# A soft-capped attention and spectral mixing kernel: weight splits and row sums of the first batch move between engines and steps, and the last batch's squares go out on two queues

## Chip, core and metric

The kernel runs on one core of a Trainium2 chip. The time is device microseconds of one execution. Five instruction streams matter: TensorE (PE, with its weight loads PEld), VectorE (DVE), ScalarE (ACT), GpSimd (POOL, nearly unused here) and SyncE (SP), which issues nearly all transfers. Each stream is executed in the order in which it is written; the streams wait for each other through semaphores.

## What is computed

```python
# q, k, v: (8 batches, 12 heads, 448 tokens, 64); x has 768 columns
scores = cap * tanh(q @ k^T / sqrt(64) / cap)
attn   = exp(scores - max) / (sum(exp(scores - max)) + 1e-9)
x      = heads side by side of (attn @ v)                   # (8, 448, 768)
theta  = x @ w_theta
zr, zi = x * cos(theta), x * sin(theta)
y      = w_tok_r @ zr + w_tok_i @ zi                         # over the tokens
u      = x + y
out    = u + max(u @ w_ch, 0)
```

## The kernel before

Attention is cut into 48 **units** of two heads, six units to a batch. A **step** s starts the scores of unit s and finishes unit s-1. Steps 0 to 7 do attention alone (table FRONT); from step 8 on, six steps do attention of one batch and, beside it, the mixing of an earlier one (PARTS, and OTHER for the first two steps and the last batch). Every step is a string of words, executed in order, and each word issues instructions on one engine or two. So the order on each engine is the order of the words. The words that matter here:

- `A`, `B`: scores of the unit's two halves on PE (lines "s", L216); both write the same PSUM tile, so `B` waits for the tanh of `A` (`tA`, L221) and the next `A` for `tB`. `eA`, `eB`: exponentials on ACT (L227). `V`: attn times v on PE (L259), with `cV` its copy on ACT (L265).
- `R`: row sums on PE by ones (L278), `I`: reciprocal on DVE (L301) and four transfers that spread it (bc, L305), `N` or `n`: the multiplications by it on DVE (L309). `aA`, `aB`: DVE adds the four 112x896 pieces of a unit's exponentials into `ps` (L249 once, L252 twice), after which `R` needs 2 matmuls for a unit instead of 8. Units under DIRECT have no such additions: units 0 to 5 are summed in pairs straight from the exponentials, units 6 up to DIRECT one at a time.
- `w0`, `w1`, `w2`: steps of the weights as listed in WEIGHTS: `>ch2` loads block 2 of w_ch, `*ch2` scales it on ACT (L110), `ch2` splits it on DVE into a high and a low part (L118 to L127; the rounding to the high part, L123, is on ACT for all blocks of w_ch).
- Mixing of column block j: `T` theta on PE (L328 to L330), `y` two copies on ACT (L350, L351), `d` three operations on DVE (L356 to L358), `sc` cosine and sine of two blocks on ACT (L363, L364; they need another function table than tanh and exp), `r` products with x on DVE (L368), `f` transposition inside 32x32 tiles on DVE (L372), `D` the **square** of two blocks: 16 transfers between partition groups inside `g_sb` (L381), `h`, `l` high and low parts of the transposed blocks on ACT and DVE (zh L386, zl L392; "a" the first four token chunks, "b" the other three), `M` the mixing matmuls (mx, 12 for "a", 9 for "b"), `m` their addition to x, `u` the split of u (us), `C` the channel matmuls (ch), `c` the last addition (L413) and the transfer of a block to the output (L414).

Square 0 goes from blocks 0 and 1 of `g_sb` to 6 and 7, square 1 from 2 and 3 to where square 0 came from, square 2 from 4 and 5 to 2 and 3. Transfers use eight landing semaphores in turn, in program order: one waits until the transfer eight before it has landed, and until what it overwrites was read.

Of the kernel before, what the change touches and what calls it, by code (L numbers as in the profile page):

```python
# [12 lines left out]
F32 = mybir.dt.float32  # L13
# [4 lines left out]
ALU = mybir.AluOpType  # L18

P = 128  # L20
# [5 lines left out]

FIRST = 8

DIRECT = 10

FILL = {"before the branch": 8, "first scores": 2, "half": 8, "slot": 10}

# [4 lines left out]
def softcap_attn_then_spectral_mix(ctx, tc, qk2, v, cap, w_theta, w_tok, w_ch, outT):  # L37
    nc = tc.nc
# [90 lines left out]
    def room_g(at):  # L129
# [3 lines left out]
            return raw, st[:, 2 * DM :].rearrange("p (j n) -> p j n", j=NJ)  # L133
        return room

    def room_t(i, name):
        def room():
            raw = g_sb[:, (12 + 2 * i) * S : (14 + 2 * i) * S]
            t = wk.tile([P, S], F32, tag="zl", name=f"{name}_t", bufs=2)
            return raw.rearrange("p (n two) -> p n two", two=2), t  # L140
        return room
# [3 lines left out]
    def weight_steps():  # L145
        for m in range(NJ):
            ms = slice(m * P, (m + 1) * P)
            steps["th", m] = Split(room_g((0, 6 * S)[m % 2]), w_theta[m], wth_h[:, :, ms], wth_l[:, :, ms])
            steps["ch", m] = Split(room_g((0, 6 * S, 8 * S, 0, 8 * S, 0)[m]), w_ch[m], wch_h[:, :, ms], wch_l[:, :, ms], True)
        for c in range(NC2):  # L150
            steps["tk", c] = Split(room_t(c % 2, f"swk{c}"), w_tok[c], wtk_h[:, c], wtk_l[:, c])

# [8 lines left out]
    }  # L161

    def weights(s, pos):
# [210 lines left out]
    def carry(b, i):  # L374

        at = 4 * S * i
        to = 4 * S * (i - 1) if i else 12 * S
        z, t = (g_sb[:, n : n + 4 * S].rearrange("p (c m d) -> p c m d", m=4, d=32) for n in (at, to))
        for m in range(4):
            for d in range(4):  # L380
                nc.sync.dma_start(t[32 * m : 32 * m + 32, :, d, :], z[32 * d : 32 * d + 32, :, m, :])  # L381

    def z_high(b, j, h):
        c0, c1 = ((0, 4), (4, NC2))[h]
# [25 lines left out]

    def chan_out(b, m):
        x = X.pop((b, m))
        nc.vector.scalar_tensor_tensor(x, acc_of.pop(("ch", b, m))[:, :S], 0.0, x, op0=ALU.max, op1=ALU.add)  # L413
        nc.sync.dma_start(outT[b, m * P : (m + 1) * P, :], x)  # L414

    FRONT = "A tA w0 eA V cV v R0 B tB R1 q w1 n I eB aA aB w2 x"
    PARTS = (
# [8 lines left out]
    )  # L426
    OTHER = {
        (0, 0): "A tA V cV w0 v R I B tB q P w1 eA T0 y0 d0 aA eB T1 y1 d1 sc0 T2 y2 r0 r1 f0 f1 d2 w2 D0",
        (0, 1): "A tA V cV N w0 v R I aB- B tB q P w1 T3 y3 d3 sc1 eA T4 r2 r3 f2 f3 D1 y4 d4 eB T5 aA aB y5 d5 w2",
        (B - 2, 4): "V cV u3 u4 u5 R I C0 c0 C1 X0 X1 c1 C2 X2 X3 c2",  # L430
        (B - 2, 5): "N X4 X5 T0+ y0+ d0+ T1+ y1+ d1+ sc0+ T2+ r0+ r1+ f0+ f1+ D0+ y2+ d2+ T3+ y3+ d3+ sc1+ T4+ r2+ r3+ f2+ f3+ D1+ y4+ d4+"
                    " T5+ y5+ d5+ sc2+ C3 c3 r4+ r5+ f4+ f5+ D2+ C4 c4 h0a+ l0a+ h0b+ l0b+ h1a+ C5 c5",
        (B - 1, 0): "M0a l1a h1b M0b l1b h2a m0 u0 M1a l2a h2b M1b l2b h3a m1 u1 M2a l3a h3b M2b l3b h4a m2 u2 M3a l4a h4b M3b l4b h5a"
                    " m3 u3 M4a l5a h5b M4b l5b m4 u4 M5a M5b m5 u5 C0 c0 C1 c1 C2 c2 C3 c3 C4 c4 C5 c5",
    }
# [1 line left out]
    def pipeline(general):  # L437
# [2 lines left out]
        load_qk(1)  # L440
        for step in (("tk", 0), ("tk", 1)):
            steps[step].load()

        def run(s, b, word):
            if word.endswith("+"):
# [23 lines left out]
            elif word == "cV":  # L469
                if done:  # L470
                    av_out(k)
            elif word == "v":
                if s + 1 < NS:
                    load_v(s + 1)
            elif name == "R":
                if done:
                    sums(k, (0, 1) if i is None else (i,))
            elif word == "I":
                if done:
                    invert(k)  # L480
            elif word == "q":
                if s + 2 <= WHOLE:
                    load_qk(s + 2)
            elif word == "P":
                if WHOLE <= s + 1 < NS:
                    prep(s + 1)
            elif name == "w":
                weights(s, "abc"[i])
            elif word == "N":
                norm(s - 3)  # L490
                norm(s - 2)
            elif word == "n":
                for n in {4: (0, 1), 5: (2, 3), 7: (4, 5)}.get(s, ()):
                    norm(n)
            elif word == "x":
                for j in {6: range(4), 7: range(4, NJ)}.get(s, ()):
                    split_x(0, j, "xs")
            elif name == "u":
                split_x(b, i, "us")
            elif name == "X":  # L500
                if b + 1 < B:
                    split_x(b + 1, i, "xs")
            elif name in ("h", "l", "M"):
                {"h": z_high, "l": z_low, "M": mix}[name](b, i, half)
            else:
                {"T": theta, "y": turns, "d": reduce, "sc": sincos, "r": rotate, "f": flip, "D": carry, "m": mix_out, "C": chan,
                 "c": chan_out}[name](b, i)
# [63 lines left out]
```

## Time and profile before

| | |
|---|---|
| three runs | 941.32, 944.65, 946.21 us (median 944.65) |
| the profiled execution | 941.22 us, its span 939.4 us, mean clock of PE 0.996 of full |
| busy share of the span | PE 98%, PEld 70%, DVE 73%, ACT 66%, POOL 0% |
| the chain that ended last | PE 73%, ACT 15%, DVE 6%, SP's queue 3%, DMA 1% |

The span is measured from the first to the last instruction; 1.8 us of the execution lie outside it. The share of the chain tells which engine the end waited for at each moment; a busy PE is nearly everywhere on it, so the places to look at are those where PE waits.

### The profile page before, as it was taken

What the parts mean: (1) busy time and instruction counts of PE and PEld (TensorE: products, weight loads), DVE (VectorE), ACT (ScalarE), POOL (GpSimd) and SP (SyncE); (2) the same over time, 40 slices, a digit from 0 to 9 for tenths busy, and PEclk for the clock granted to TensorE, in tenths of its full rate; (3) what the DMA queues carried; (4) which work ended last, traced back from release to release, by engine and by line L of the source; (5) the groups of instructions that cost most, each with busy time, mean ns of one, the idle gap of its engine ahead of it and who ended that gap; (6) DMA issues with size and microseconds to landing.
All of it is one profiled execution on the core that took longest, in us unless ns stands there. A gap on an engine that the chain in (4) does not pass through costs nothing.

```text
span 939.4 us, 12874 instructions
## 1 busy us (share of the span) xinstructions
PE 916.8 (98%) x4912; PEld 660.9 (70%) x4912; DVE 682.9 (73%) x914; ACT 617.6 (66%) x644; POOL 0.4 (0%) x6
## 2 busy tenths in 40 slices
PE   8999989999999999999999999999999999999997
PEld 4224657667776787777677776776877777789887
DVE  5898756997876679666887568775787568965741
ACT  7988696567954688656976479645895569753420
POOL 0000000000000000000000000000000000000000
PEclk9999999999999999999999999999999999999999
DMA  7664155422642235332452325422353333411521
GB/s 267 200 186 128 34 123 132 121 98 72 126 89 79 82 65 120 78 108 70 86 102 67 101 62 107 117 78 71 67 119 80 91 96 76 77 32 48 92 52 62
DMA packets 208774, 90.66 MB, mean 97 GB/s; under 512 B 182464, under 2 KB 194752, under 8 KB 208704
## 3 DMA queue, kind: packets, MB, share of 16 engines
q1 hardware_dynamic: 208704, 89.76, 38.3%
q8 instruction: 40, 0.66, 0.3%
q14 instruction: 30, 0.25, 0.1%
HBM read 45.68 MB, written 11.01 MB: 60 GB/s over the span
## 4 chain that ended last, share of the span: by engine, by line
PE 73%; ACT 15%; DVE 6%; SPq 3%; DMA 1%; issue 1%; DVEq 0%; ACTq 0%
PE a L259 10%; PE s L216 10%; PE mx L403 7%; PE mx L401 7%; PE mx L402 7%; PE ch L328 6%; PE ch L329 6%; PE ch L330 6%; ACT p L221 5%; PE th L328 4%; PE th L329 4%; PE th L330 4%; SPq L381 3%; ACT p L227 2%; PE r L278 2%; ACT L221 2%
## 5 line engine op out<-in xcount | busy, mean ns | idle before, releaser
L221 ACT ACTIVATE p<-s,qscale 112x1792 f32<-112x1792 f32 x96 | 168.5, 1755 | 124.2 <-PE s L216 122.6
L227 ACT ACTIVATE p<-p,cap_sb 112x1792 f32<-112x1792 f32 x96 | 170.2, 1785 | 0.4
L259 PE MATMUL a<-p,v 112*64 112x448 f32 x768 | 155.1, 546 | 3.7 <-ACT p L227 3.7
L259 PEld LDWEIGHTS a<-p,v 112*64 112x64 f32 x768 | 50.7, 136 | 91.0 <-issue 74.9
L328 PE MATMUL ch<-us,wch_h 128*128 128x448 f32 x288 | 107.1, 372 | 0.0
L328 PE MATMUL th<-xs,wth_h 128*128 128x448 f32 x288 | 107.0, 371 | 0.0
L329 PE MATMUL ch<-us,wch_h 128*128 128x448 f32 x288 | 105.5, 366 | 0.0
L329 PE MATMUL th<-xs,wth_h 128*128 128x448 f32 x288 | 105.5, 366 | 0.0
L330 PE MATMUL ch<-us,wch_l 128*128 128x448 f32 x288 | 105.4, 366 | 0.0
L330 PE MATMUL th<-xs,wth_l 128*128 128x448 f32 x288 | 105.3, 366 | 0.0
L252 DVE TENSOR_TENSOR ps<-ps,p 112x896 f32<-112x896 f32 x76 | 82.8, 1089 | 2.2
L301 DVE RECIPROCAL ri<-r 128x448 f32<-128x448 f32 x24 | 70.9, 2954 | 17.2 <-PE r L278 17.2
L403 PE MATMUL mx<-wtk_h,zl_False 128*128 128x448 f32 x192 | 71.4, 372 | 3.2 <-DVE zl_False L392 2.5
L401 PE MATMUL mx<-wtk_h,zh_False 128*128 128x448 f32 x192 | 72.0, 375 | 0.1
L402 PE MATMUL mx<-wtk_l,zh_False 128*128 128x448 f32 x192 | 70.2, 366 | 0.0
L368 DVE TENSOR_TENSOR g_sb<-g_sb,x 128x896 f32<-128x896 f32 x48 | 50.7, 1086 | 22.3 <-ACT g_sb L364 22.3
L413 DVE SCALAR_TENSOR_TENSOR x<-ch,x 128x448 f32<-128x448 f32 x48 | 29.8, 620 | 51.1 <-PE ch L330 51.1
L328 PEld LDWEIGHTS ch<-us,wch_h 128*128 128x128 f32 x288 | 54.2, 188 | 10.3 <-issue 5.3
L328 PEld LDWEIGHTS th<-xs,wth_h 128*128 128x128 f32 x288 | 54.1, 188 | 9.6 <-issue 5.2
L330 PEld LDWEIGHTS ch<-us,wch_l 128*128 128x128 f32 x288 | 54.2, 188 | 4.9 <-DVE wch_l L127 0.2
L330 PEld LDWEIGHTS th<-xs,wth_l 128*128 128x128 f32 x288 | 54.1, 188 | 4.7
L329 PEld LDWEIGHTS th<-xs,wth_h 128*128 128x128 f32 x288 | 54.1, 188 | 4.6 <-DVE xs L320 0.3
(79 smaller groups left out, 1550.8 us busy)
## 6 DMA issues: line engine op xcount, KB each, us to landing
g_sb<-g_sb SPq DMA_DIRECT2D x384, 56.0 KB, 2.0
qk_sb<-in_qk SPq DMA_DIRECT2D x35, 448.0 KB, 3.6
v<-in_v SPq DMA_DIRECT2D x48, 224.0 KB, 2.9
bc<-ri SPq DMA_DIRECT2D x96, 112.0 KB, 2.3
out_dram<-x SPq DMA_DIRECT2D x48, 224.0 KB, 2.0
qk<-in_qk SPq DMA_DIRECT2D x13, 448.0 KB, 3.5
g_sb<-in_wth SPq DMA_DIRECT2D x6, 768.0 KB, 5.7
g_sb<-in_wch SPq DMA_DIRECT2D x6, 768.0 KB, 4.8
```

The source lines that it names most:

```text
L216: nc.tensor.matmul(sp[:CP, i, hh, :S], kk[k][rows, 1, ks], qq[k][rows, 0, :], start=n == 0, stop=n == len(products) - 1)
L221: nc.scalar.activation(pt[k, half], spt.pop((k, half))[:CP, :, :, :S], AF.Tanh, scale=qscale[:CP])
L227: nc.scalar.activation(pp, pp, AF.Exp, scale=cap_sb[:CP])
L252: nc.vector.tensor_tensor(pst[k], pst[k], pt[k, 1][:, i], op=ALU.add)
L259: nc.tensor.matmul(acc[hh * D : (hh + 1) * D, :S], va[:, hh, c, :], pt[k, c // 2][:, c % 2, hh, :], start=c == 0, stop=c == NCH - 1)
L301: nc.vector.reciprocal(ri, r[:, :S])
L328: nc.tensor.matmul(acc[:, :S], wh[:, j, ms], t[:, 0, :], start=j == 0, stop=False)
L329: nc.tensor.matmul(acc[:, :S], wh[:, j, ms], t[:, 1, :], start=False, stop=False)
L330: nc.tensor.matmul(acc[:, :S], wl[:, j, ms], t[:, 0, :], start=False, stop=j == NJ - 1)
L401: nc.tensor.matmul(acc[:, :S], zh, wtk_h[:, c, :], start=c == 0, stop=False)
L402: nc.tensor.matmul(acc[:, :S], zh, wtk_l[:, c, :], start=False, stop=False)
L403: nc.tensor.matmul(acc[:, :S], zl, wtk_h[:, c, :], start=False, stop=c == NC2 - 1)
```

## The change

In the first batch the row sums of units 8 and 9 are prepared by additions on DVE (DIRECT 10 to 8). Row sums of units 1 and 3 (with 0 and 2) are finished, inverted and used one step later than before. The splits of blocks 1 and 2 of w_ch do their rounding on DVE instead of ACT, block 2 gets a room of its own, is loaded a step earlier (step 10) and is scaled and split at the head of step 11 instead of at its end; blocks 3, 4 and 5 swap rooms. In step 9 the words `eA`, `eB` and `aB-` come earlier. In the last batch, `h0a l0a h0b l0b h1a` come before `C3`, half of squares 1 and 2 (every odd d) is issued on ACT's queue, and the very last output block is added and sent in two halves, one on each queue.

```diff
-DIRECT = 10
+DIRECT = 8
+    def room_x(name):
+        def room():
+            raw = wk.tile([P, 4 * S], F32, tag="xhl", name=f"{name}_raw", bufs=3)[:, : 2 * DM]
+            st = g_sb[:, 12 * S : 12 * S + DM]
+            return raw.rearrange("p (j n two) -> p j n two", j=NJ, two=2), st.rearrange("p (j n) -> p j n", j=NJ)
+        return room
...
-            steps["ch", m] = Split(room_g((0, 6 * S, 8 * S, 0, 8 * S, 0)[m]), w_ch[m], wch_h[:, :, ms], wch_l[:, :, ms], True)
+            steps["ch", m] = Split(room_x("swc2") if m == 2 else room_g((0, 6 * S, None, 8 * S, 0, 8 * S)[m]), w_ch[m], wch_h[:, :, ms],
+                                     wch_l[:, :, ms], m not in (1, 2))
...
-        (8, "b"): "tk5", (8, "c"): "*tk6 tk6 *ch1", (9, "a"): "ch1", (11, "b"): ">ch2",
-        (11, "c"): ">ch3 *ch2 ch2 >ch4", (12, "b"): "*ch3 ch3 >ch5", (12, "c"): "*ch4 ch4", (13, "b"): "*ch5 ch5",
+        (8, "b"): "tk5", (8, "c"): "*tk6 tk6 *ch1", (9, "a"): "ch1", (10, "a"): ">ch2", (11, "a"): "*ch2 ch2", (11, "b"): ">ch3",
+        (11, "c"): ">ch4", (12, "b"): "*ch3 ch3 >ch5", (12, "c"): "*ch4 ch4", (13, "b"): "*ch5 ch5",
...
-                nc.sync.dma_start(t[32 * m : 32 * m + 32, :, d, :], z[32 * d : 32 * d + 32, :, m, :])
+                queue = nc.scalar if b == B - 1 and i and d % 2 else nc.sync
+                queue.dma_start(t[32 * m : 32 * m + 32, :, d, :], z[32 * d : 32 * d + 32, :, m, :])
...
-        nc.vector.scalar_tensor_tensor(x, acc_of.pop(("ch", b, m))[:, :S], 0.0, x, op0=ALU.max, op1=ALU.add)
-        nc.sync.dma_start(outT[b, m * P : (m + 1) * P, :], x)
+        acc = acc_of.pop(("ch", b, m))
+        last = b == B - 1 and m == NJ - 1
+        for at, queue in ((slice(0, S // 2), nc.sync), (slice(S // 2, S), nc.scalar)) if last else ((slice(0, S), nc.sync),):
+            nc.vector.scalar_tensor_tensor(x[:, at], acc[:, at], 0.0, x[:, at], op0=ALU.max, op1=ALU.add)
+            queue.dma_start(outT[b, m * P : (m + 1) * P, at], x[:, at])
...
-        (0, 1): "A tA V cV N w0 v R I aB- B tB q P w1 T3 y3 d3 sc1 eA T4 r2 r3 f2 f3 D1 y4 d4 eB T5 aA aB y5 d5 w2",
+        (0, 1): "A tA N V cV v R I B tB eA aB- w0 q P w1 T3 eB y3 d3 sc1 T4 r2 r3 f2 f3 D1 y4 d4 aA T5 aB y5 d5 w2",
...
+        def late(s):
+            return not general and 2 <= s < 6
...
             elif name == "R":
-                if done:
+                if late(s) and i == 1:
+                    if s % 2:
+                        sums(k - 1, (1,))
+                elif done:
                     sums(k, (0, 1) if i is None else (i,))
             elif word == "I":
-                if done:
+                if late(s):
+                    if s % 2:
+                        invert(k - 1)
+                elif done:
                     invert(k)
...
-                for n in {4: (0, 1), 5: (2, 3), 7: (4, 5)}.get(s, ()):
+                when = {4: (0, 1), 5: (2, 3), 7: (4, 5)} if general else {5: (0, 1), 6: (2, 3), 7: (4, 5)}
+                for n in when.get(s, ()):
                     norm(n)
```

**PE in steps 9 and 10**, before: the scores and attn-times-v of units 9 and 10, with the sums of unit 8 (from p_0_603 and p_1_639) and of unit 9 after each V. These are the rows of step 9 and then of step 10, with the theta matmuls between them left out after the first piece.

```order
L216 MATMUL s_0_759<-qk_575 112x448 x4
L259 MATMUL a_766<-p_0_603,v_557 64x448 x4
L259 MATMUL a_766<-p_1_639,v_557 64x448 x4
L278 MATMUL r_788<-p_0_603,ones_sb 32x448 x4
L278 MATMUL r_788<-p_1_639,ones_sb 32x448 x4
L216 MATMUL s_1_797<-qk_575 112x448 x4
```

Now, step 10, where the sums of both units stand between V of unit 9 and the second half of unit 10's scores; step 9 has none.

```order
L224 MATMUL s_0_901<-qk_645 112x448 x4
L267 MATMUL a_908<-p_0_762,v_620 64x448 x4
L267 MATMUL a_908<-p_1_784,v_620 64x448 x4
L286 MATMUL r_935<-ps_679,ones_sb 32x448 x2
L286 MATMUL r_935<-ps_873,ones_sb 32x448 x2
L224 MATMUL s_1_940<-qk_645 112x448 x4
```

So 16 matmuls of these two units became 4, and the last two of them read ps_873, which DVE makes in step 9.

**DVE at the end of step 9**, before: the last three operations `d5` and the low parts of the first transposed block, which M0 reads, come straight after `d4`.

```order
L356 SCALAR_TENSOR_TENSOR g_sb<-g_sb 128x448
L357 TENSOR_SCALAR g_sb<-g_sb 128x448
L358 TENSOR_SCALAR g_sb<-g_sb 128x448
L392 TENSOR_TENSOR zl_0_False<-g_sb,zh_0_False 128x512
L392 TENSOR_TENSOR zl_0_True<-g_sb,zh_0_True 128x384
```

Now, from the end of `d4`:

```order
L366 TENSOR_SCALAR g_sb<-g_sb 128x448
L257 TENSOR_TENSOR ps_873<-p_0_762 112x896
L260 TENSOR_TENSOR ps_873<-ps_873,p_1_784 112x896 x2
L364 SCALAR_TENSOR_TENSOR g_sb<-g_sb 128x448
L365 TENSOR_SCALAR g_sb<-g_sb 128x448
L366 TENSOR_SCALAR g_sb<-g_sb 128x448
L401 TENSOR_TENSOR zl_0_False<-g_sb,zh_0_False 128x512
L401 TENSOR_TENSOR zl_0_True<-g_sb,zh_0_True 128x384
```

Three additions of unit 9 stand ahead of `d5` and of the low parts.

**ACT in the last batch**, before, from `sc1` to the high parts (th_4 and th_5 are `y4` and `y5`):

```order
L364 ACTIVATE g_sb<-g_sb 128x2x448
L350 ACTIVATE g_sb<-th_4_6955 128x448
L351 ACTIVATE g_sb<-g_sb 128x448
L350 ACTIVATE g_sb<-th_5_6999 128x448
L351 ACTIVATE g_sb<-g_sb 128x448
L363 ACTIVATE g_sb<-g_sb,quarter 128x2x448
L364 ACTIVATE g_sb<-g_sb 128x2x448
L386 CAST zh_0_False<-g_sb 128x512
L386 CAST zh_0_True<-g_sb 128x384
L386 CAST zh_1_False<-g_sb 128x512
L386 CAST zh_1_True<-g_sb 128x384
```

Now:

```order
L390 DMA g_sb<-g_sb 32x14x32 x8
L358 ACTIVATE g_sb<-th_4_6952 128x448
L359 ACTIVATE g_sb<-g_sb 128x448
L358 ACTIVATE g_sb<-th_5_6996 128x448
L359 ACTIVATE g_sb<-g_sb 128x448
L371 ACTIVATE g_sb<-g_sb,quarter 128x2x448
L372 ACTIVATE g_sb<-g_sb 128x2x448
L395 CAST zh_0_False<-g_sb 128x512
L395 CAST zh_0_True<-g_sb 128x384
L395 CAST zh_1_False<-g_sb 128x512
L390 DMA g_sb<-g_sb 32x14x32 x8
L395 CAST zh_1_True<-g_sb 128x384
```

The eight transfers of square 1 stand between `sc1` and `y4`, the eight of square 2 between `h1a` and `h1b`.

## Rows read from the trace of the kernel before

**Rows 1.** The view of waits of PE, first two rows of the stretch 100 to 180 us, the third of 850 to 940 us. Columns: who waited for whom, us in total, times, longest us.

```profile
PE a L259 <- ACT p L227: 3.7, 2, 2.7
PE s L216 <- ACT p L221: 1.7, 1, 1.7
...
PE mx L403 <- DVE zl_False L392: 2.5, 2, 1.5
```

**Rows 2.** The timeline of 68 to 88 us (end of the attention-only steps). Columns: start us, us, engine, line, operation, tiles, shapes, count, and in brackets the idle time of the engine before it and what ended it.

```profile
68.57 2.96 DVE L301 RECIPROCAL ri<-r 128x448 f32<-128x448 f32 x1 [0.24 <-PE r L278]
...
78.95 0.84 ACT L123 CAST wch_h<-g_sb 128x768 fp32r<-128x768 f32 x1
...
80.81 3.23 PE L259 MATMUL a<-p,v 112*64 112x448 f32 x16
...
83.95 1.75 ACT L221 ACTIVATE p<-s,qscale 112x1792 f32<-112x1792 f32 x1
...
87.10 1.76 PE L216 MATMUL s<-qk 64*112 64x448 f32 x8
```

**Rows 3.** The timeline of steps 9 and 10 (104 to 135 us), columns as in rows 2.

```profile
104.85 3.20 PE L278 MATMUL r<-p,ones_sb 112*32 112x448 f32 x16
106.08 1.75 ACT L221 ACTIVATE p<-s,qscale 112x1792 f32<-112x1792 f32 x1
...
107.98 1.76 PE L216 MATMUL s<-qk 64*112 64x448 f32 x8
...
114.11 0.84 ACT L123 CAST wch_h<-g_sb 128x768 fp32r<-128x768 f32 x1 [5.86 <-DVE g_sb L119]
...
125.36 1.72 PE L259 MATMUL a<-p,v 112*64 112x448 f32 x8 [2.72 <-ACT p L227]
...
126.25 1.77 ACT L227 ACTIVATE p<-p,cap_sb 112x1792 f32<-112x1792 f32 x1
...
131.86 0.55 DVE L392 TENSOR_TENSOR zl_True<-g_sb,zh_True 128x384 fp32r<-128x384 f32 x1
...
132.87 1.76 PE L216 MATMUL s<-qk 64*112 64x448 f32 x8
```

**Rows 4.** The view of waits of DVE, 106 to 132.5 us, columns as in rows 1.

```profile
DVE g_sb L356 <- ACT g_sb L351: 2.5, 2, 1.3
DVE g_sb L368 <- ACT g_sb L364: 1.9, 1, 1.9
DVE zl_False L392 <- ACT zh_False L386: 0.7, 1, 0.7
```

**Rows 5.** The view of groups of instructions over the whole span, shapes kept apart. Columns: line, engine, operation, tiles, shapes, count, busy us, mean ns of one, idle us before and what ended it.

```profile
L252 DVE TENSOR_TENSOR ps<-ps,p 112x896 f32<-112x896 f32 x76 | 82.8, 1089 | 2.2
...
L125 DVE CAST wth_h<-g_sb 128x768 fp32r<-128x768 f32 x6 | 3.4, 562 | 0.0
```

**Rows 6.** The timeline of steps 11 and 12 (157 to 178 us), columns as in rows 2.

```profile
157.18 0.69 DVE L392 TENSOR_TENSOR zl_False<-g_sb,zh_False 128x512 fp32r<-128x512 f32 x1 [2.86 <-DMA bc<-ri]
...
167.19 1.76 PE L216 MATMUL s<-qk 64*112 64x448 f32 x8
...
172.04 0.96 PE L278 MATMUL r<-ps,ones_sb 112*32 112x448 f32 x8
...
172.12 0.84 ACT L123 CAST wch_h<-g_sb 128x768 fp32r<-128x768 f32 x1 [4.64 <-DVE g_sb L119]
...
174.66 3.00 PE L216 MATMUL s<-qk 64*112 64x448 f32 x8 [1.66 <-ACT p L221]
```

**Rows 7.** The view by stretches. Columns: the stretch in us, its length, busy us and instructions of PE, PEld, DVE, ACT and POOL, granted clock of PE as a share of full speed, busy share of the DMA engines, GB/s.

```profile
175.00:178.40 3.40, 3.40 (x10) 1.41 (x7) 3.40 (x5) 2.06 (x5) 0.00 (x0) 0.50 0.48 128
```

**Rows 8.** The timeline of the last batch (866 to 906 us), columns as in rows 2. The row of 866.33 holds the 32 transfers of squares 0 and 1, that of 889.01 those of square 2.

```profile
866.33 21.92 SPq L381 DMA_DIRECT2D g_sb<-g_sb  x32
...
870.84 0.52 ACT L350 ACTIVATE g_sb<-th 128x448 f32<-128x448 f32 x1
...
875.00 0.58 DVE L356 SCALAR_TENSOR_TENSOR g_sb<-g_sb 128x448 f32<-128x448 f32 x1
...
877.43 0.39 DVE L358 TENSOR_SCALAR g_sb<-g_sb 128x448 int32<-128x448 int32 x1
...
879.65 0.60 ACT L386 CAST zh_False<-g_sb 128x512 fp32r<-128x512 f32 x1
879.78 2.09 DVE L368 TENSOR_TENSOR g_sb<-g_sb,x 128x896 f32<-128x896 f32 x2 [1.42 <-ACT g_sb L364]
...
884.32 0.67 DVE L392 TENSOR_TENSOR zl_False<-g_sb,zh_False 128x512 fp32r<-128x512 f32 x1
...
889.01 10.62 SPq L381 DMA_DIRECT2D g_sb<-g_sb  x16
...
901.43 0.62 ACT L386 CAST zh_False<-g_sb 128x512 fp32r<-128x512 f32 x1 [5.11 <-DMA g_sb<-g_sb]
```

**Rows 9.** The view of line L381 in 850 to 905 us: how long one issue of a square's transfer holds SP's queue (ns, smallest, median, largest), and the time from issue to landing.

```profile
L381 SPq DMA_DIRECT2D g_sb<-g_sb x48: 585/623/1109, 866.3 to 899.0; - x48
...
DMA to landing us min/median/max: 2.0/2.0/3.2
```

**Rows 10.** The chain that ended last, in order of time: one of the mixing matmuls. Columns: start us, us, what.

```profile
890.00 0.21 PE mx L402
```

More of the change, by code (lines that the diff above doesn't have):

```diff
@@ L428, in softcap_attn_then_spectral_mix @@
         (0, 0): "A tA V cV w0 v R I B tB q P w1 eA T0 y0 d0 aA eB T1 y1 d1 sc0 T2 y2 r0 r1 f0 f1 d2 w2 D0",
-        (0, 1): "A tA V cV N w0 v R I aB- B tB q P w1 T3 y3 d3 sc1 eA T4 r2 r3 f2 f3 D1 y4 d4 eB T5 aA aB y5 d5 w2",
+        (0, 1): "A tA N V cV v R I B tB eA aB- w0 q P w1 T3 eB y3 d3 sc1 T4 r2 r3 f2 f3 D1 y4 d4 aA T5 aB y5 d5 w2",
         (B - 2, 4): "V cV u3 u4 u5 R I C0 c0 C1 X0 X1 c1 C2 X2 X3 c2",
         (B - 2, 5): "N X4 X5 T0+ y0+ d0+ T1+ y1+ d1+ sc0+ T2+ r0+ r1+ f0+ f1+ D0+ y2+ d2+ T3+ y3+ d3+ sc1+ T4+ r2+ r3+ f2+ f3+ D1+ y4+ d4+"
-                    " T5+ y5+ d5+ sc2+ C3 c3 r4+ r5+ f4+ f5+ D2+ C4 c4 h0a+ l0a+ h0b+ l0b+ h1a+ C5 c5",
+                    " T5+ y5+ d5+ sc2+ h0a+ l0a+ h0b+ l0b+ h1a+ C3 c3 r4+ r5+ f4+ f5+ D2+ C4 c4 C5 c5",
         (B - 1, 0): "M0a l1a h1b M0b l1b h2a m0 u0 M1a l2a h2b M1b l2b h3a m1 u1 M2a l3a h3b M2b l3b h4a m2 u2 M3a l4a h4b M3b l4b h5a"
```

## Prediction

> **What bounds the kernel now.** I read the busy shares first: PE is busy nearly all the time and stands on the chain almost everywhere, so what the change is worth is decided where PE waits or would wait. Then the waits of PE in the two regions that the change touches [rows 1]: in steps 9 to 12 it waits 3.7 us for exponentials before V of unit 9 and 1.7 us for a tanh in step 12; in the last batch 2.5 us in two waits for a low part (1.5 before M0, so 1.0 before M4). That is 7.9 us. Last the timelines around these waits, to see what makes each late.
>
> V of unit 9 is late since ACT, behind `tA`, stood idle 5.86 us until DVE had come to block 1 of w_ch; only then could the rounding on ACT, and behind it `tB` and the exponentials, go on [rows 3]. In step 12 it is the same with block 2: the rounding at 172.12 stands ahead of `tA`, and after the wait PE's eight score matmuls took 3.00 us instead of 1.76 [rows 3, 6], because its clock was granted at 0.50 from 175.0 to 178.4 [rows 7]. M0 waits for the low part that DVE ends at 884.99, M4 for `h4a` at 901.43, which waited for square 2 to land [rows 8].
>
> **The change, part by part.**
>
> *Steps 2 to 7.* The same work, some of it a step later. PE loses nothing: the sums moved from behind one `B` to behind the next stand in a wait for `tB` in both places. On DVE the reciprocals no longer fill the wait for a scaled block at 34 us and fill a shorter one at 43 us, so by my adding up the third reciprocal ends 0.9 us later than 71.53 [rows 2]. ACT's rounding of block 0 waits for DVE and moves from 78.95 to about 79.8, the exponentials behind it end near 82.4, just when V of unit 7 (from 80.81, 3.23 long) comes to its second half; the next `tA`, 0.9 later, ends at 86.6, before 87.10 where PE wants it [rows 2]. I cost it at nothing; the cover is used up, and anything more is lost one for one (up to 1 us).
>
> *Steps 9 and 10.* Removed from PE: 3.20 us of sums in each of two steps [rows 3], for 0.5 us of them after (half of the 0.96 that a prepared pair takes [rows 6] hangs on the last addition). Both waits for exponentials (3.7) go too. But `B` of step 9 starts at 107.98 right behind `tA`, which ends at 107.83 [rows 3], and `tA` does not move: the sums of unit 8 leave a hole there. And DVE gets more: before, it ended the low parts of the first block at 132.41 after waiting 2.5, 1.9 and 0.7 us on the way [rows 3, 4]. It now gets two additions of unit 8, three of unit 9 (1.09 each) and a rounding (0.56) [rows 5], 6.0 us together. They fill the waits of 2.5 and 0.7, but not that of 1.9, which is the sines that follow `d3` directly. So DVE ends at 132.41 + 6.0 - 3.2 = 135.2, and the additions of unit 9, 2.6 us before that, at 132.6. PE, through V at 125.7, waits 7 us for them in `R`, then `B` runs from 133.1: +0.25 against 132.87. In that hole I expect the clock to fall as it did around a wait of 1.66 us [rows 6, 7]; that half-speed stretch cost 1.24 us on the scores and some on what followed, half of 3.4 us: +1.7. It could also cost nothing (the waits of 2.7 and 1.0 at 122 to 128 left the clock alone) or twice that.
>
> *Step 11.* The split of block 2 now stands between the additions of unit 10 and `l4a`. DVE was idle from 154.3 to 157.18 there [rows 6]; the split takes 5.6 us (the 5.0 between 170.5 and 175.5, with 0.56 for the rounding), so with the 0.25 above `l4a` ends at 160.85. PE wants it at the third matmul of M4, 40 matmuls of 0.21 us [rows 10] before 167.19 [rows 6], 158.9, or 159.15 now: +1.7.
>
> *Step 12.* The tanh is free: -1.66, and the slow scores -1.24. First batch together: 0.25 + 1.7 + 1.7 - 2.9 = +0.75.
>
> *Last batch.* ACT never issued a transfer before, so its price has no row. The nearest is SP's: 0.62 us an issue, 0.585 to 1.109 [rows 9], 0.685 with the steps between (21.92 / 32) [rows 8]. The lower bound is nearly nothing. I take 0.685, for it is the same transfer. What is queued behind matters more: `y4`, at 870.84 [rows 8], now stands behind the eight transfers of square 1. They wait for the transposition (875.1), and the fourth of them for the sixteenth of square 0 to land, which SP issues at 866.33 + 15 x 0.685 = 876.6 and which lands 2.0 us later [rows 8, 9], 878.6. ACT is through at 878.6 + 5 x 0.685 = 882.0. Then `y4` 1.1, `d4` and `d5` 2.8 (875.00 to 877.82), the sines 1.8 (877.82 to 879.65), `h0a` 0.6, `l0a` 0.67 [rows 8]: 889.1 instead of 884.99. Bringing the halves ahead of `C3` takes off the products that stood before them, and this is counted here.
>
> Then `l0b` 0.55, `c3` 0.6, products 2.09 and transpositions 2.1: square 2 can start at 894.5, not 889.0. ACT holds its half until 894.5 and issues until 900.0, and `h1b` stands behind: 900.5, its low part 901.1. The third matmul of M1's second half reads it; M0's third was at 885.05, 33 matmuls earlier, so it would have run at 891.9. That is 9.2 later. The wait of 1.0 at M4 is gone (square 2 lands by 902.5, M4 comes after 909): +8.2. PE stands still over 4 us before it, so I add a fall of the clock here too, +1.7, with nothing as the other bound. If issuing on ACT were free, ACT would be through at 878.6, `l0a` at 885.7, square 2 start at 891.1; the fifth of ACT's eight then waits for the first to land (893.1), the low part comes at 894.2: 2.3 - 1.0 = +1.3.
>
> Here a rule of the Trainium skill speaks the other way. Rows 9 show SP's queue held by 48 issues of 0.62 us, and square 2's 10.62 us of issuing end just before `h4a` can run [rows 8]. The Trainium skill, Perfetto Trace Analysis, section DMA Optimizations, says that where issuing is the bottleneck, spreading transfers over the engines that can issue them may help. By that rule square 2 would go out in half the time and both waits of the last batch would go, -2.5; by the rows, ACT's own work stands behind the transfers, and the sum is +8.2.
>
> *The end.* One addition (0.62) and one transfer become two of each, the second pair on ACT's idle queue: two shorter additions cost about what the halved transfer saves. Zero, 0.3 either way.
>
> **Sum.** 0 + 0.75 + 8.2 + 1.7 = +10.65 on 941.2: 951.9. The profiled execution lies 3.4 below the median of the runs, so the median would be up to 955; I say 953.
>
> **Rivals.**
> 1. *Issuing on ACT is nearly free.* Against it: it is the same transfer as SP's. For it: no row of ACT. Then the last batch costs 1.3, without a fall of the clock: 941.2 + 0.75 + 1.3 = 943.2, or 946.7 from the median. No difference to be told.
> 2. *The queues do what they look made for* (not slower): the transfers do not hold `y4` and `h1b`. It decides whether `y4` can still run before 874; the order on ACT speaks against it, since it stands behind. Then the last batch gains both waits, -2.5, and without a fall of the clock the first -0.95: 937.7, or 941.2 from the median.
> 3. *Two queues press on the same DMA engines, and every hidden delay shows.* The clock falls twice in each place and the front loses its 1 us: 941.2 + 10.65 + 1 + 3.4 = 956.3, 959.7 from the median.
>
> **How the numbers follow.** Chances: my sum 0.66, rival 1 0.18, rival 2 0.07, rival 3 0.09. The range that leaves out 2 in 10 reaches from rival 1 taken from the profiled execution, 943, to rival 3, 959; my sum's own is 948 to 956. About 0.5% (4.7 us) is what can be told from no change: under 939.9 lies a part of rival 2 (0.05), within 0.5% the rest of it and rival 1 (0.20), above 949.4 the others (0.75).
>
> **What the next profile would show.** Right: PE waits about 7 us in step 10 for an addition on DVE, and the clock falls there; no wait for a tanh in step 12, a wait under 2 us for `l4a` in step 11; ACT's `y4` of the last batch after 878 and not near 871; eight issues of 0.6 us in ACT's stream; `h1b` behind square 2, and PE waiting over 4 us before M1's second half. Wrong: issues on ACT far shorter than SP's, `y4` before 874, or the additions of unit 9 done before V ends.

## The result and the profile after

The changed kernel takes 956.46 us (median of five, 951.40 to 956.91) against 944.65 before (median of five, 941.32 to 946.21): ratio 1.0114, interval 1.008 to 1.0148. It is slower by 11.8 us; 953 was forecast, in a range of 943 to 959. The profiled execution took 956.91 us with a span of 955.1.

The head of the page of the changed kernel: PE's share of the span falls from 98% to 96%, DVE and ACT have about as much to do as before.

```profile
PE 920.8 (96%) x4888; PEld 663.2 (69%) x4888; DVE 689.5 (72%) x923; ACT 616.6 (65%) x642; POOL 0.4 (0%) x6
```

The waits of PE in the changed kernel, 100 to 200 us and then 860 to 930 us (who waited for whom, us in total, times, longest):

```profile
PE r L286 <- DVE ps L260: 5.6, 1, 5.6
PE s L224 <- ACT p L229: 3.0, 1, 3.0
PE mx L412 <- DVE zl_False L401: 1.4, 1, 1.4
...
PE ch L336 <- ACT g_sb L358: 2.9, 1, 2.9
PE mx L410 <- ACT zh_True L395: 2.4, 1, 2.4
PE mx L412 <- DVE zl_False L401: 2.1, 1, 2.1
PE mx L410 <- ACT zh_False L395: 2.0, 1, 2.0
```

All three waits of [rows 1] are gone, and seven others stand there: 10.0 us in the first batch where 5.4 stood, 9.4 in the last where 2.5 stood. The timeline of PE in the changed kernel puts them in their places.

```profile
112.03 2.63 PE L224 MATMUL s<-qk 64*112 64x448 f32 x8 [2.95 <-ACT p L229]
...
137.90 1.71 PE L286 MATMUL r<-ps,ones_sb 112*32 112x448 f32 x4 [5.58 <-DVE ps L260]
139.53 3.33 PE L224 MATMUL s<-qk 64*112 64x448 f32 x8
...
169.04 0.47 PE L412 MATMUL mx<-wtk_h,zl_False 128*128 128x448 f32 x1 [1.38 <-DVE zl_False L401]
...
177.40 1.76 PE L224 MATMUL s<-qk 64*112 64x448 f32 x8
...
183.13 1.76 PE L224 MATMUL s<-qk 64*112 64x448 f32 x8
...
888.96 0.47 PE L336 MATMUL ch<-us,wch_h 128*128 128x448 f32 x1 [2.92 <-ACT g_sb L358]
894.90 0.47 PE L410 MATMUL mx<-wtk_h,zh_False 128*128 128x448 f32 x1 [2.01 <-ACT zh_False L395]
902.28 0.47 PE L412 MATMUL mx<-wtk_h,zl_False 128*128 128x448 f32 x1 [2.11 <-DVE zl_False L401]
906.99 0.47 PE L410 MATMUL mx<-wtk_h,zh_True 128*128 128x448 f32 x1 [2.40 <-ACT zh_True L395]
```

Set against the rows of before, the same work starts later by: `B` of step 9 4.05 us (107.98, [rows 3], to 112.03), `B` of step 10 6.66 (132.87 to 139.53), `A` of step 12 10.21 (167.19, [rows 6], to 177.40), `B` of step 12 8.47 (174.66 to 183.13), SP's first transfer of the last squares 6.54 (866.33, [rows 8], to 872.87), the end 15.7 (939.4 to 955.1). So the two traces part in three places: 4.1 us before step 9, some 2.5 in steps 9 to 12, and 9.2 in the last batch.

The last batch on ACT and DVE, changed kernel, 875 to 907 us (ACTq is the issuing of transfers by ACT):

```profile
876.54 0.94 ACT L372 ACTIVATE g_sb<-g_sb 128x896 f32<-128x896 f32 x1
881.69 6.63 ACTq L390 DMA_DIRECT2D g_sb<-g_sb  x8
888.37 0.54 ACT L358 ACTIVATE g_sb<-th 128x448 f32<-128x448 f32 x1 [10.89 <-DMA g_sb<-g_sb]
...
889.55 0.62 DVE L364 SCALAR_TENSOR_TENSOR g_sb<-g_sb 128x448 f32<-128x448 f32 x1 [7.94 <-ACT g_sb L359]
...
894.88 0.69 DVE L401 TENSOR_TENSOR zl_False<-g_sb,zh_False 128x512 fp32r<-128x512 f32 x1 [2.46 <-ACT zh_False L395]
...
900.67 5.66 ACTq L390 DMA_DIRECT2D g_sb<-g_sb  x8
906.42 0.51 ACT L395 CAST zh_True<-g_sb 128x384 fp32r<-128x384 f32 x1 [10.64 <-DMA g_sb<-g_sb]
```

`y4` starts at 888.37, 881.83 in the time of before (the 6.54 us by which the squares start later taken off), where it started at 870.84 [rows 8]. ACT stands still for 10.89 us in front of it: 4.2 of them until the transposition of blocks 2 and 3 (the first transfer waits for it), 6.6 for the issuing of the eight. DVE stands still for 7.94 us behind `y4`. The same happens to `h1b` behind square 2.

### The profile page after: what moved, and what is told of

Same layout as the page of the kernel before. It is cut to its first block, busy times and chain, and to the rows that moved or that the text cites. A ratio compares the mean times of both kernels' runs of the same rounds, so it can differ in the third digit from the quotient of the medians.

```text
span 955.1 us, 12839 instructions
## 1 busy us (share of the span) xinstructions
PE 920.8 (96%) x4888; PEld 663.2 (69%) x4888; DVE 689.5 (72%) x923; ACT 616.6 (65%) x642; POOL 0.4 (0%) x6
## 5 line engine op out<-in xcount | busy, mean ns | idle before, releaser
L260 DVE TENSOR_TENSOR ps<-ps,p 112x896 f32<-112x896 f32 x80 | 87.1, 1089 | 2.3
L425 DVE SCALAR_TENSOR_TENSOR x<-ch,x 128x448 f32<-128x448 f32 (+1 forms) x49 | 29.7, 610 | 51.1 <-PE ch L338 51.1
L364 DVE SCALAR_TENSOR_TENSOR g_sb<-g_sb 128x448 f32<-128x448 f32 x48 | 29.5, 615 | 43.5 <-ACT g_sb L359 43.5
L224 PE MATMUL s<-qk 64*112 64x448 f32 x208 | 49.7, 600 | 9.9 <-ACT p L229 9.8
```

The source lines that it names most:

```text
L260: nc.vector.tensor_tensor(pst[k], pst[k], pt[k, 1][:, i], op=ALU.add)
```

## The experiments

Times are medians beside runs of the kernel before on the same chip. The last three columns are worked out from the traces, against the trace of before: **front**, how much later the first scores of step 9 start (100.00 us before; the expectations call the stretch from here on steps 8 to 13); **first**, what is added from there to the first scores of step 13; **last**, what is added from the end of the last theta matmul to the end.

| run | us | ratio to before (95%) | front | first | last |
|---|---|---|---|---|---|
| changed kernel | 956.5 | 1.0114 (1.008 to 1.0148) | +4.2 | +2.7 | +9.2 |
| e1 before + odd d on ACT | 960.2 | 1.0154 (1.0131 to 1.0177) | +0.2 | 0.0 | +16.2 |
| e2 before + whole last batch | 955.7 | 1.0095 (1.0065 to 1.0126) | +3.9 | +0.2 | +10.4 |
| e3 changed first batch only | 946.0 | 1.0022 (1.0004 to 1.0039) | +2.0 | +3.0 | +0.1 |
| e4 changed, squares on SP | 945.8 | 1.0011 (0.9993 to 1.0029) | +2.0 | +1.7 | +1.6 |
| e5 splits moved, sums on PE | 941.1 | 0.9960 (0.9945 to 0.9975) | +3.2 | -4.0 | +0.4 |
| e6 sums of units 8, 9 on DVE | 947.1 | 1.0021 (1.0007 to 1.0035) | +3.4 | +2.0 | +0.5 |
| e7 before + odd d on POOL | 942.4 | 0.9980 (0.9968 to 0.9993) | +2.0 | -1.3 | -1.3 |
| e8 before + ACT in pieces | 942.5 | 0.9977 (0.9962 to 0.9992) | +6.1 | +0.2 | -1.6 |
| e9 made to be the best | 941.4 | 0.9969 (0.9948 to 0.9990) | +3.4 | -5.5 | -1.7 |
| e10 changed, POOL for ACT | 944.3 | 1.0000 (0.9984 to 1.0015) | +4.0 | +2.8 | -2.6 |
| e11 changed, y4 y5 sc2 first | 952.3 | 1.0079 (1.0056 to 1.0102) | +2.2 | +3.1 | +4.4 |
| e12 e5 + odd d on POOL | 937.9 | 0.9938 (0.9915 to 0.9961) | | | |

Where nothing was edited, a stretch still differs from trace to trace, as the clock falls in one of its waits or not: **front** from +0.2 to +6.1 in e1, e2, e7 and e8, **first** from -1.3 to +0.2 in the same four, **last** from +0.1 to +0.5 in e3, e5 and e6.

### The second queue, alone and with the rest of the last batch

e1 makes one edit in the kernel before:

```diff
-                nc.sync.dma_start(t[32 * m : 32 * m + 32, :, d, :], z[32 * d : 32 * d + 32, :, m, :])
+                queue = nc.scalar if b == B - 1 and i and d % 2 else nc.sync
+                queue.dma_start(t[32 * m : 32 * m + 32, :, d, :], z[32 * d : 32 * d + 32, :, m, :])
```

> The kernel before, with one edit: every odd d of squares 1 and 2 of the last batch is issued on ACT's queue; the order of the words stays. Theory A (what stands behind the transfers in ACT's order decides): y4 stands behind square 1's eight transfers and runs 11 us later than before, as in the changed kernel; and because the halves h0a and h0b here stand behind square 2 in the order, ACT holds them too until it has issued eight more. Worked out: y4 at 882.0, sc2 through at 888, products and transpositions to 892, ACT issuing until 897.6, l0a at 899 instead of 885; less the 1.0 us wait of M4 that goes: +12.8 us, up to +14.5 if the clock falls in the hole, a median of 957 to 959. That is more than the whole change cost in its last batch (+9.2 in its trace). Theory B (a second queue shortens the issuing and costs nothing else): both waits of the last batch go, -2.5 us, a median near 942. Theory C (the two queues press on the same DMA engines): the time from issue to landing rises well over the 2.0 us of before.

e2 adds the other edits of the last batch (the halves ahead of `C3`, the last output in two halves) and nothing of the first.

> The kernel before, with all three edits of the last batch (halves ahead of C3, odd d on ACT's queue, the last output in two halves) and none of the first batch. Theory A: the last batch costs here what it cost in the trace of the changed kernel, about +9 us from the first theta matmul of the last batch to the end, whatever the first batch does; a median of 953 to 955, and a front like that of the kernel before. If instead the loss of the changed kernel sits in its first 110 us (its trace lies 4.2 us behind there) and the last batch only adds to it by accident, this kernel stays within 4 us of before.

Measured: 960.22 and 955.70 us. The waits of PE in e1, 860 to 930 us:

```profile
PE mx L402 <- ACT zh_False L387: 9.8, 1, 9.8
PE ch L328 <- ACT g_sb L350: 4.2, 1, 4.2
```

The edit of one line costs 16.2 us, more than the whole change; theory A had 12.8 to 14.5, and the median of 960.2 lies over its 957 to 959. The two waits less the old ones come to 11.5; the rest is the clock, which fell behind both holes: 0.50 granted from 881.5 to 888.2 us, 0.52 from 891.2 to 905.2. The mechanism is as forecast: without the halves ahead of `C3`, `h0a` stands behind both squares. e2 gives back the last batch of the changed kernel with the first batch of before; its +10.4 holds two falls of the clock (0.50 granted from 886.4 to 893.2 and from 906.9 to 910.3), the +9.2 of the changed kernel one (from 908.1 to 911.5). Theory B (two queues simply halve the issuing) falls. So does C: the time from issue to landing is 2.1 us in the median in e1 and in the changed kernel, against 2.0 [rows 9].

### The first batch alone, and the squares back on SP

e3 is the changed kernel with the last batch as before; e4 is the changed kernel with one line taken back (the line above).

> The changed kernel with the last batch put back as before (order, one queue, one last transfer). The trace of the changed kernel lies behind that of before by 4.2 us at 100 us, by 7.0 after step 12 and by 6.5 at 840 us. Theory A1: the 4.2 us of the front come from how the execution started (half-speed first scores and one fall of the clock, ahead of any edit) and not from the edits: the trace shows a front of +0 to +4 as it falls out, steps 9 to 12 cost +2 to +3, and the median is 945.5 to 948. Theory A2: they come from the later sums of units 1 and 3: the front costs 4 us in this kernel too, median 950 to 952. Step 11 has a wait for l4a of 1.4 us, step 12 none for a tanh, in both.

> The changed kernel with all squares on SP's queue again; the halves stay ahead of C3 and the last output stays in two halves. Theory A: y4 is back at its place (about 871 in the time of the trace of before), the wait of M0 for its low part goes (-1.45), and the two low parts that now stand ahead of r4 start square 2 about 1.2 us later, so that h4a and with it M4 come 1.2 us later than before, whatever M0 gained: 1.2 us over the run without any edit of the last batch, and 8 us under the changed kernel, a median of 947 to 950. If the halves ahead of C3 and not the second queue made the loss, this kernel stays at 955 to 957.

Measured: 945.96 and 945.81 us. The first batch costs +1.7 to +3.0 us in these traces, and the second queue nearly all of the rest: one line takes the changed kernel from 956.5 to 945.8, under the 947 to 950 that was expected. e4's last batch costs +1.6 where +1.2 was worked out, but not in the way worked out. Square 2 starts 17.14 us after the last theta matmul (892.57 less 875.43) where it started 16.84 after it before (889.01 less 872.17), so `l0a` and `l0b` ahead of `r4` make it only 0.3 later; PE's waits come to 2.8 us where 2.5 stood. The rest is a fall of the clock behind them. The stretch in e4 (columns as in rows 7):

```profile
907.10:910.50 3.40, 3.13 (x8) 2.81 (x9) 1.85 (x4) 0.57 (x1) 0.00 (x0) 0.50 0.00 0
```

The front settles for A1. It is +2.0 in both of these, though both have the later sums of units 1 and 3, and +3.9 in e2, which has not. And from the second half of the first unit's scores (9.14 us before, 11.10 in e3, 11.09 in e4) to the first scores of step 9 (100.00, 101.99, 101.97) the three kernels take 90.86, 90.89 and 90.88 us: the later sums cost nothing there.

### The parts of the first batch

e5 takes the splits of blocks 1 and 2 and the new order of step 9 into the kernel before, and leaves the sums of units 8 and 9 on PE (`DIRECT` 10). e6 does the reverse: `DIRECT = 8` and the new order alone.

> The kernel before with the rounding of blocks 1 and 2 of w_ch on DVE, block 2's own room and earlier place, and the new order of step 9; the row sums of units 8 and 9 stay on PE (DIRECT 10), and neither the later sums of units 1 and 3 nor any edit of the last batch is made. Theory A (the additions of units 8 and 9 made the holes of steps 9 and 10, and the rest of the first batch is a gain): the 3.2 us of sums of unit 8 fill the wait of B of step 9, the exponentials of unit 9 are there when V comes, so the waits of 2.7 and 1.0 go, and step 12 keeps its gain of 2.9 to 3.4; step 11's wait for l4a (1.4) stays or grows by what PE comes earlier. -2 to -6 us, a median of 938 to 942, and no hole of 5.6 us. Theory B (the sums on PE only hide the same late chain, and M0 or M4 wait instead): the waits of 3.7 us come back as waits of the mixing matmuls, and the median is 943 to 945.

> The kernel before with the row sums of units 8 and 9 prepared on DVE (DIRECT 8) and the new order of step 9, and nothing else of the change. Theory A: this part alone makes the holes: about 3 us before B of step 9 and 5 to 6 us before the sums of step 10, whose price in the runs with the whole first batch was +2.5 (no fall of the clock at the first hole) to +4.5 us (two falls) between the start of step 8 and that of step 11; step 12's tanh wait stays. Median 946.5 to 948.5. Theory B (the additions cost nothing, the move of the splits does): no hole over 2 us in step 10, median 941 to 944.

Measured: 941.06 and 947.11 us. The waits of PE, 100 to 200 us, first in e5, then in e6:

```profile
PE mx L411 <- DVE zl_False L400: 1.4, 1, 1.4
PE mx L409 <- ACT zh_False L394: 1.1, 1, 1.1
```

```profile
PE r L278 <- DVE ps L252: 5.0, 1, 5.0
PE s L216 <- ACT p L221: 4.6, 2, 3.0
```

In e5 the sums keep PE busy where the changed kernel has its holes, the waits for exponentials and for the tanh of step 12 are gone, and no wait as long takes their place; the granted clock of PE is 1.00 from 100 to 180 us. In e6 both holes are there. So in the first batch the gain came from the splits and the order (which of the two, no run tells apart), and moving PE work that stood in a wait to DVE gave it away: of 3.20 us of sums taken from each of two steps, none came back as time.

### A queue with nothing behind it, and a queue used in pieces

e7 puts `nc.gpsimd` in the place of `nc.scalar` in e1. e8 leaves square 1 on SP and gives ACT the eight odd transfers of square 2, two behind each of four halves (`E0` to `E3`, m from 0 to 3), with the halves ahead of `C3`:

```diff
+            for d in (1, 3):
+                nc.scalar.dma_start(t[32 * m : 32 * m + 32, :, d, :], z[32 * d : 32 * d + 32, :, m, :])
...
-        (B - 1, 0): "M0a l1a h1b M0b l1b h2a m0 u0 M1a l2a h2b M1b l2b h3a m1 u1
+        (B - 1, 0): "M0a l1a h1b E0 M0b l1b h2a E1 m0 u0 M1a l2a h2b E2 M1b l2b h3a E3 m1 u1
```

> The kernel before with every odd d of squares 1 and 2 of the last batch on POOL's queue, which has nothing else to do; ACT issues nothing. Theory A (what stands behind the transfers on ACT costs the time, not the second queue as such): no wait for y4; the wait of M0 is as before (1.45), square 2 is issued in half the time, so the 1.0 us wait of M4 goes: -1 us, a median of 942.5 to 944, if an issue on POOL holds its queue about as long as one of SP's. Theory C (two queues at once slow each other, or an issue on POOL is much slower): square 2 lands later than before, M4 waits longer than 1.0, and the time is above that of before.

> The kernel before with the halves of blocks 0 and 1 ahead of C3 as in the change, square 1 on SP alone, and the eight odd transfers of square 2 on ACT's queue, but two at a time behind h1b, h2a, h2b and h3a, so that ACT's own work is held by 1.3 us at a time and stands ahead of the rest. Theory A: the same second queue now pays: M0's wait of 1.45 goes, square 2 ends some 4 us earlier and M4's wait of 1.05 goes too, no other wait over 0.5 us: -2 to -2.5 us, a median of 941.5 to 942.5. If issuing on ACT's queue costs time wherever it stands, the halves run late and the median is 945 or more.

Measured: 942.43 and 942.52 us, each less than 0.1 us outside what was expected; last batches -1.3 and -1.6. The line of the transfers in e7 (how long one issue holds its queue in ns, smallest, median, largest) and from issue to landing:

```profile
L382 SPq DMA_DIRECT2D g_sb<-g_sb x32: 585/622/1587, 867.6 to 890.1; - x32
L382 POOL DMA_DIRECT2D g_sb<-g_sb x16: 632/638/892, 877.0 to 897.6; - x16
...
DMA to landing us min/median/max: 2.0/2.2/3.7
```

An issue costs 638 ns on POOL, 622 on SP, and 646 on ACT in the changed kernel: the price is nearly the same on the three queues, and what differs is what stands behind. The Trainium skill, DMA: Bandwidth & Descriptors, section Issuing engines are not separate DMA queues, says that issuing from several engines saves only the time of issuing; here the time to landing stays at 2.0 to 2.2 us, which agrees.

e8's last batch came out up to 0.9 us short of its forecast, by the same mechanism in small. ACT and DVE of e8 around 898 us:

```profile
897.01 0.62 ACT L393 CAST zh_False<-g_sb 128x512 fp32r<-128x512 f32 x1 [4.40 <-PE mx L410]
897.03 1.31 ACTq L388 DMA_DIRECT2D g_sb<-g_sb  x2
898.38 0.57 ACT L319 CAST us<-x 128x448 fp32r<-128x448 f32 x1 [0.75 <-issue]
...
898.98 0.63 DVE L320 TENSOR_TENSOR us<-x,us 128x448 fp32r<-128x448 f32 x1 [3.45 <-ACT us L319]
899.52 0.68 DVE L399 TENSOR_TENSOR zl_False<-g_sb,zh_False 128x512 fp32r<-128x512 f32 x1
```

`u0` on ACT stands behind two transfers, its second part on DVE waits for it, and the low part that M2 reads stands behind that: PE waits 1.1 us for it.

### The changed kernel with one thing put right, and two tries at a better one

e10 exchanges ACT's queue for POOL's in the changed kernel; e11 keeps ACT's queue and moves `D1` behind `y4 d4 T5 y5 d5 sc2`.

> The changed kernel with one name exchanged: the odd d of squares 1 and 2 go to POOL's queue and not to ACT's. Theory A: all of the last batch's loss goes, and its two waits too: from the end of the theta matmuls to the end -1.5 to -2.5 us against the kernel before, where the changed kernel has +9.2; the first batch stays at +1.5 to +3. Median 943 to 946, 11 to 13 under the changed kernel. If two queues as such cost time, it stays above 950.

> The changed kernel with square 1's transfers moved behind y4, y5 and sc2 in the order, ahead of h0a: ACT still issues its half of both squares. It parts the loss of the last batch into that of square 1 (through y4) and that of square 2 (through h1b). Theory A: y4 runs at 871 (in the time of the kernel before) and C5 no longer waits for it; ACT issues square 1's half from 880 to 885, so l0a comes at 886.3, 1.3 later than before; square 2 starts at 892, h1b at 898, which M1 wants at 893: from the end of the theta matmuls to the end +5 to +7 us against before, where the changed kernel has +9.2; a median of 951 to 954.

Measured: 944.26 and 952.31 us, both medians inside what was expected (e11's last batch with +4.4 just under its 5 to 7). So of the 9.2 us, 4.8 came through `y4` behind square 1 and 4.4 stay with `h0a` and `h1b` behind the transfers; with the same transfers on POOL the last batch is 2.6 faster than before, and of its two old waits (2.5) only 0.5 is left.

e9 joins e5, POOL's queue and the halves ahead of `C3`, and splits block 2 at the end of step 11; e12 joins e5 and e7 alone.

```diff
-        (11, "a"): "*ch2 ch2", (11, "b"): ">ch3", (11, "c"): ">ch4",
+        (11, "a"): "*ch2", (11, "b"): ">ch3", (11, "c"): "ch2 >ch4",
```

> A version meant to beat both: the run with the moved splits and the new order of step 9 (row sums of units 8 and 9 on PE), with block 2 split at the end of step 11 and not at its head, and in the last batch the halves ahead of C3 and the odd d of squares 1 and 2 on POOL's queue. Theory A: steps 8 to 13 gain 4.0 us as in the run with the splits alone, the wait for l4a of 1.4 us in step 11 goes, and the waits of M0 and M4 of the last batch go (-2.5): -6 to -8 us under the kernel before, a median of 936 to 938.5. If the split at the end of step 11 makes the tanh of step 12 wait again, 1.7 to 2.9 of it are lost.

> The run with the moved splits and the new order of step 9, with the odd d of squares 1 and 2 on POOL's queue and the words of the last batch as before. Theory A: the two gains add: -4.0 in steps 8 to 13 and -1.3 in the last batch, a median of 939 to 941 beside one of 944 to 946 for the kernel before; step 11 keeps its wait of 1.4 and M0 of the last batch its wait of 1.45, which tells, beside the run that takes both away, whether they are worth their 2.8 us.

e12 is the best, 937.9 us, 0.6% under the kernel before and 1.1 us under the 939 to 941 expected. (Its profiled execution, of 3517 us, is left out, so no stretches can be given; the other eight lie between 935.5 and 941.6.) e9, with 941.4 us, missed its 936 to 938.5: the wait for `l4a` in step 11 went as forecast, and came back later. ACT of e9, 187 to 195 us:

```profile
192.43 0.83 ACT L123 CAST wch_h<-g_sb 128x768 fp32r<-128x768 f32 x1 [4.09 <-DVE g_sb L119]
193.17 1.75 ACT L229 ACTIVATE p<-s,qscale 112x1792 f32<-112x1792 f32 x1
```

DVE, later by the split of block 2, comes later to blocks 3 and 4; their rounding still is on ACT, ahead of the tanh of step 13, and PE waits 2.95 us for that. From step 13 to the end of the theta matmuls e9 loses 4.2 us, of the 7.2 that it gains in the two other stretches (-5.5 and -1.7). It is the old wait of step 12, one step on. A fall of the clock behind the wait makes up the rest: 0.72 granted in the mean from 194 to 200 us.

## Why the prediction was right, and where it was off

**Step 9.** Right: `tA` did not move (110.22 in the changed kernel, 106.1 in the time of before), and `B` waits 2.95 us where the sums had been.

**Step 10.** Right in kind: PE waits for the additions of unit 9. The term was too small. I let the six additions and the rounding fill DVE's waits of 2.5 and 0.7 us [rows 4]; but the 2.5 is two waits of 1.3, and the first, ahead of `d3`, is for `y3`, which itself waits for the end of DVE's split. It moves along and is never filled. The timeline of the changed kernel, first ACT's `y3`, then DVE's `d3`, the additions of unit 9 and `d5`:

```profile
124.50 0.55 ACT L358 ACTIVATE g_sb<-th 128x448 f32<-128x448 f32 x1 [4.67 <-DVE wch_l L127]
...
125.68 0.62 DVE L364 SCALAR_TENSOR_TENSOR g_sb<-g_sb 128x448 f32<-128x448 f32 x1 [1.28 <-ACT g_sb L359]
...
135.62 2.22 DVE L260 TENSOR_TENSOR ps<-ps,p 112x896 f32<-112x896 f32 x2
137.76 0.62 DVE L364 SCALAR_TENSOR_TENSOR g_sb<-g_sb 128x448 f32<-128x448 f32 x1
```

`d3` still waits 1.28 us, `d5` no longer. So the additions end 1.1 us later than summed: 133.7 in e4 (135.67 less its front of 1.97) against 132.6. Nor do the sums of one unit take half of a pair's 0.96: those of unit 8 took 0.95 alone (131.37 to 132.32). The rest is the clock. I had one fall at 1.7; the trace of the changed kernel has two, one behind each hole, and only the second counts. PE, slowed by the first, comes later to the second hole and waits less there: 5.58 us, where e4, without the first fall, waits 7.19 for the same addition.

```profile
135.73 1.71 PE L286 MATMUL r<-ps,ones_sb 112*32 112x448 f32 x4 [7.19 <-DVE ps L260]
```

`B` of step 10 starts 35.4 us after `A` of step 9 in both (139.53 less 104.16, 137.36 less 101.97). The second fall makes the sums of unit 9 1.71 us long in both, and the scores behind them 3.33 in the changed kernel instead of 1.76. How much it costs follows from how much of PE's work it covers. The stretches of that fall in e4, the changed kernel and e11 (columns as in rows 7; the number behind the length is PE's busy time, all of it at a clock of 0.50):

```profile
132.30:139.10 6.80, 3.37 (x10) 1.06 (x12) 5.79 (x9) 4.79 (x7) 0.00 (x0) 0.50 0.51 85
137.90:143.50 5.60, 5.60 (x14) 1.92 (x15) 2.42 (x5) 1.88 (x2) 0.00 (x0) 0.50 0.54 90
132.20:142.30 10.10, 6.42 (x16) 2.66 (x17) 6.04 (x9) 5.05 (x8) 0.00 (x0) 0.50 0.51 85
```

With 3.4, 5.6 and 6.4 us of work at half clock the whole first batch costs 1.7, 2.7 and 3.1 us. By these three, as an estimate, it would cost about nothing without that fall; the trace of before, beside which this is counted, has a fall of its own in step 12. From `A` of step 9 to `A` of step 11 the changed kernel takes 52.0 us instead of 47.6: 4.4 more, for the 0.25 + 1.7 forecast.

**Step 11.** Right: `l4a` late by the split, 1.38 us of waiting and 1.65 to `A` of step 12, for 1.7 forecast.

**Step 12.** Right: no wait for a tanh, no half-speed scores; between `A` and `B` of step 12 1.74 us come back and behind `B` 1.61, of which the scores are 1.24, for 2.9 forecast. The second part was luck: of the six traces with this wait of 1.66 us the scores behind it are slow in two, before and e1; in e2, e6, e7 and e8 they take 1.76. The first batch in all: +2.7 to step 13 and +2.4 by the last squares, for +0.75.

**Last batch.** Right in size, +9.2 for 8.2 + 1.7, and in its links: `y4` at 881.8 in the time of before (882.0 forecast), `l0a` through at 889.0 (889.1), square 2 at 894.1 (894.5), `h1b` through at 900.4 (900.5). That ACT would stop before its fourth issue, for the landing of square 0, is not to be seen in the trace; the eight issues come one after another, 0.83 us each with what lies between. The fall of the clock that was added came too, 0.50 granted from 908.1 to 911.5. Where PE waits was not right: I put all of it before M1's second half and overlooked a resource. `C5` writes the PSUM buffer that `T4` wrote, and cannot start before `y4` has read it, so 2.9 us of the delay show there; 2.0 show at M0, 2.1 at M1's low part, which stands behind `r4` to `c5` on DVE, and only 2.4 at `h1b`. The sum is the same, since each wait takes off what the next would have been.

**The end.** Right: nothing. From PE's last matmul to the end it is 5.1 us before (934.28 to 939.4), in the changed kernel (949.99 to 955.1) and in e10 (937.93 to 943.0).

**The rivals.** That issuing on ACT is nearly free fell: 646 ns. That the queues do what they look made for fell on ACT and holds on POOL (e7, e10). Of the third, the press on the DMA engines fell (2.1 us to landing, for 2.0), and the clock fell once in the last batch. The rule that the prediction quotes from the Trainium skill, Perfetto Trace Analysis, section DMA Optimizations, was right about the bottleneck and wrong for this queue, with ACT's own work behind the transfers: -2.6 us by e10, +9.2 by the changed kernel. A second queue alone takes away the 1.05 us of M4 only: in e7, which leaves the words as they were, M0 still waits 1.46 us, and in e4, which has the halves ahead of `C3` and one queue, 0.42. So the one wait goes with the queue and the other with the order of the words.

**The front.** Costed at nothing. The trace of the changed kernel loses 4.2 us there, but so does that of e2 (3.9), which has no edit there, and e1 loses 0.2. The profiled execution of before had neither the slow start nor a fall there, and it lies 3.4 us under its median. By the medians the change costs 11.8; first batch and last batch by the trace give 2.4 + 9.2 = 11.6. The sum had 0.75 + 8.2 + 1.7 = 10.65, so part of the fit is luck: the first batch cost 1.65 more than forecast, the last 0.7 less.

## What to carry to other kernels

A transfer issued on ACT's queue held ACT here not only for the 0.6 us of issuing but for everything that the first transfer waited for (10.89 us for eight). Before a second queue is used, read what stands behind the transfers in that engine's order: on a queue with nothing behind it the same transfers gained 1.3 us (2.6 with the halves ahead of `C3`) where they had cost 16.2 (9.2), and half of them, in pieces behind the work that PE wants next and with the halves ahead of `C3`, gained 1.6 on ACT's queue. And work on PE that stood in a wait was free: taking it away shortened nothing, left holes in which the clock fell, and loaded the engine that the second hole waits for.

## What the runs showed of the hardware

**Whether the clock falls in a hole is not settled by the hole's length.** The same hole of 2.95 us before `B` of step 9 is in six of the traces; the clock fell behind it in the changed kernel, e3, e6 and e10, and not in e4 and e11. The rows of 110 to 115 us (columns as in rows 7), first e3, then e4:

```profile
110.00:115.00 5.00, 5.00 (x17) 3.32 (x18) 4.83 (x10) 3.26 (x3) 0.00 (x0) 0.66 0.00 0
```

```profile
110.00:115.00 5.00, 5.00 (x25) 3.69 (x26) 4.83 (x10) 3.56 (x3) 0.00 (x0) 1.00 0.00 0
```

In the same 5 us PE got through 17 matmuls in the one and 25 in the other; the fall cost some 1.5 us, which the next hole took back. The holes of 5 to 7 us before the sums of step 10 ended in a fall in all six. The waits of the kernel before were as uncertain: behind the 1.66 us in step 12 the clock fell in two of the six traces that have it (before and e1, not e2, e6, e7 and e8), and the waits of 1.9 us in steps 2 to 6 ended in a fall ten times out of 39 in the 13 traces.

**The first scores take nearly twice as long in nine of 13 traces.** They start at 6.31 us and take 3.33 in the changed kernel; in the kernel before they start at 5.52 and take 1.76. (The view by stretches gives 1.00 for both, but the trace's record of the granted clock begins only at 10.38 us in the changed kernel and at 4.36 in the kernel before. In all 13 traces the scores that start before the record are the slow ones; that they ran at half clock is likely by this, and not shown.) The first row is of the changed kernel, the second of the kernel before:

```profile
6.31 3.33 PE L224 MATMUL s<-qk_sb 64*112 64x448 f32 x8
```

```profile
5.52 1.76 PE L216 MATMUL s<-qk_sb 64*112 64x448 f32 x8
```

Of 13 traces four have the short scores; the other nine have 3.0 to 3.3 and are 1.8 to 2.8 us behind the kernel before at the next scores, and eight lose 1.7 or 3.3 more by falls of the clock in the waits ahead of steps 2 and 4, whichever kernel it is. The front of +0.2 to +6.1 us that comes of it is of the size of what executions of one kernel differ by (5.5 us between the changed kernel's fastest and slowest), and reason enough to cost an edit by its own stretch and not by the span.
